# Dense K and Q projections with the padding done by DMA, scores taken from the next pass, and V in three-tile banks

## The chip, the cores and the metric

The kernel runs on one core of a Trainium2 chip. The metric is the device time of one execution in microseconds (us). The kernel before takes 915.73 us, the median of 3 runs (915.34 to 917.61). The engines have short names here: PE is TensorE (matmuls), ACT is ScalarE, DVE is VectorE, POOL is GpSimd, SP is SyncE, which here only issues DMAs.

## The reference

The input x has 2048 tokens of 640 features. The output adds to x the product of an attention branch and a gated branch, both fed by the layer norm of x. The attention has 32 heads of 20 features.

```python
def _A_ref(x, wqkv, wo):
    B, S, D = x.shape
    H = 32; Dh = D // H
    qkv = (x @ wqkv).reshape(B, S, 3, H, Dh).transpose(2, 0, 3, 1, 4)
    q, k, v = qkv[0], qkv[1], qkv[2]
    scores = jnp.einsum("bhqd,bhkd->bhqk", q, k) * Dh ** -0.5
    p = softmax(scores, axis=-1)
    o = jnp.einsum("bhqk,bhkd->bhqd", p, v)
    return o.transpose(0, 2, 1, 3).reshape(B, S, D) @ wo
...
h = sigmoid(xn @ w_gate) * (xn @ w_up)      # 1728 features
g = silu(h @ w_down)
return x + _A_ref(xn, wqkv, wo) * g
```

There are 32 x 2048 x 2048 exponentials to take, some 134 million, against matmuls that are small by comparison, since a head has only 20 features.

## The kernel before, in words

**Layout.** Tokens lie in 16 tiles of 128. xnT holds the normalised x transposed: features on the partitions (5 tiles of 128), tokens along the row. The queries are worked in 4 chunks of 512 and the heads in 8 groups of 4. A *pass* is one chunk of queries with one group of heads, so there are 32 passes. Within a pass the scores of 16 key tiles and 4 heads are computed: 64 *banks*, each a matmul of 128 keys by 512 queries that fills one PSUM bank of 512 f32 columns. The whole kernel has 2048 such banks.

**Padding.** A matmul on 32 of PE's 128 rows works on one head, and four of them run beside each other. So each head gets a strip of 32 partitions: the first row of the strip holds a constant (1 on the side of K, and on the side of Q a bound on the score that keeps the exponentials in range), then 20 rows of features, then 11 rows of zeros. Before the change the padding is in the weights: wkp and wqp hold 32 heads of 32 columns, made on POOL (line 206), and K (line 108) and Q (line 143) are projected group by group, 128 padded columns for 4 heads of 20. The output projection (lines 614, 646) likewise takes the normalised products oT group by group with a padded wo_pad: 8 matmuls for a half of 320 columns. The bound of a group is a matmul with the absolute values of Q (absq, line 127) and the maxima of K (line 121) as weights (line 501).

**The exponentials.** Two engines make them. ACT takes the scores from two PSUM sets, one of 3 banks and one of 2, in turn (line 901); an exponential there is one instruction for the whole set. DVE takes single banks from a *spare* PSUM bank and makes the exponential from integer and cubic steps in four instructions (lines 912, 917, 921, 925: dy, du, du, p), with two buffers for dy and one for du. The probabilities p then go as moving operand into the product with V (line 999), which sums into the PSUM tile oacc, with a column of ones for the softmax's denominator. At a pass's end DVE copies oacc to oev (line 667), POOL's DMAs carry the denominators through DRAM and back, and DVE multiplies (oT, line 696).

**The gated branch.** Gate and up matmuls (lines 541, 554), a tanh on ACT (line 548) for the sigmoid, the down projection (line 576), a tanh (td, line 587) for the silu, and a store to DRAM; out jobs (line 614) read it back (gqr, line 609, four buffers) and add the result onto x in DRAM by an accumulating DMA from POOL. For the last chunk, part jobs (line 646) sum the first six groups before the end, and the last two are added after the last pass.

**What sets the order.** The order of all engines after the setup is planned when the kernel is built, by a loop that keeps its own clock for PE, ACT and DVE. ACT's sets come first: issue() (line 935) lets PE score the next banks as soon as a set is free, or just before ACT would run dry; when DVE has little queued it also gives DVE the next bank, except for the last 6 banks of a pass. Between scores PE does products with V (pv_batch) and *jobs*: K, Q, V, gate and up, down, out and part jobs, each with a due time counted in banks (lines 711 and 725 on), two in flight at most, in two PSUM banks (misc0, misc1) that also serve as spare. A job that is overdue is done before the next scores (must_fill). A zero matmul onto oacc (line 984) fills PE where it would otherwise be idle for long. Changing from one kind of PE work to another is booked with a time of its own (INTO). Every engine executes its instructions strictly in the planned order, and so does SP its DMAs: one that waits holds up those behind it. An SP DMA also waits until the eighth before it has landed.

**The setup** (the first 32 us) loads x, takes the norm, transposes, and projects K of the first group, Q of the first pass and V of four token tiles (16 heads each, line 133, ps_v); a list scheduler orders it.

Of the kernel before, what the change touches and what calls it, by code (L numbers as in the profile page):

```python
# [8 lines left out]
FP32 = mybir.dt.float32  # L9
# [5 lines left out]
P = 128  # L15
HEAD = 32
# [5 lines left out]
V_CHUNKS = ((0, 16), (16, 32))  # L22
# [17 lines left out]
def kernel(  # L40
# [26 lines left out]
    HH = HEAD // 2  # L67
    assert D == 640 and S == 2048 and Dh == 20 and HH * Dh == HALF
# [18 lines left out]
    mk_all = const.tile([P, NG, 4], FP32, name="mk_all")  # L87
    mk = const.tile([P, NG], FP32, name="mk")
    bound = const.tile([P, NG, P], BF16, name="bound")
# [7 lines left out]
    wqp = persist.tile([P, KD, HEAD, 32], BF16, name="wqp")  # L97
    wo_pad = persist.tile([P, NG, D], BF16, name="wo_pad")
# [4 lines left out]
    wkp = ep.tile([P, KD, HEAD, 32], BF16, name="wkp")  # L103
    wv = ep.tile([P, KD, D], BF16, name="wv")

    def k_matmuls(ps, g, cols):
        for kd in range(KD):
            nc.tensor.matmul(ps, lhsT=wkp[:, kd, GH * g:GH * g + GH, :].rearrange("p h e -> p (h e)"),  # L108
                             rhs=xnT[:, kd, cols],
                             start=(kd == 0), stop=(kd == KD - 1))  # L110
            yield

    def k_bound(g):
        k_most(g)
        nc.vector.tensor_scalar(out=bound[:, g, :], in0=esum, scalar1=mk[:, g:g + 1], scalar2=None, op0=ALU.mult)

    def k_most(g):
        nc.vector.tensor_reduce(out=mk[:, g:g + 1], in_=mk_all[:, g, :], axis=AXISX, op=ALU.max)

    def k_max(src, g, c):  # L120
        nc.vector.tensor_reduce(out=mk_all[:, g, c:c + 1], in_=src, axis=AXISX, op=ALU.max,
                                apply_absolute_value=True)

    def q_abs(ps):
        absq = wk.tile([P, QC], BF16, tag="absq", bufs=1, name="absq")
# [5 lines left out]
    def v_matmuls(ps, tt, h0, h1):  # L131
        for kd in range(KD):
            nc.tensor.matmul(ps[:, 0:(h1 - h0) * Dh], lhsT=xnT[:, kd, tt * P:(tt + 1) * P],  # L133
                             rhs=wv[:, kd, h0 * Dh:h1 * Dh], start=(kd == 0), stop=(kd == KD - 1))
            yield

    def v_copy(copy, ps, tt, h0, h1):
        copy(out=v_all[:, tt, h0:h1, 1:1 + Dh],
             in_=ps[:, 0:(h1 - h0) * Dh].rearrange("p (h e) -> p h e", e=Dh))

    def q_matmuls(ps, cols, g):
        for kd in range(KD):
            nc.tensor.matmul(ps, lhsT=wqp[:, kd, GH * g:GH * g + GH, :].rearrange("p h e -> p (h e)"),  # L143
                             rhs=xnT[:, kd, cols],
                             start=(kd == 0), stop=(kd == KD - 1))
            yield

# [3 lines left out]
    with tc.tile_pool(name="setup", bufs=1) as sp, \  # L153
            tc.tile_pool(name="ps0", bufs=1, space=bass.MemoryType.PSUM) as ps0:
        x_sb = sp.tile([P, TT, D], BF16, name="x_sb")
        wk_raw = sp.tile([P, KD, D], BF16, name="wk_raw")
        wq_raw = sp.tile([P, KD, D], BF16, name="wq_raw")
# [20 lines left out]
        load_w(wk_raw, 1)  # L178
        load_x(12, 4)
        load_w(wq_raw, 0)  # L180
# [5 lines left out]
        nc.gpsimd.memset(v_all[:, :, 0:HH, 0:1], 1.0)  # L186
        make_identity(nc, ident)
        nc.vector.memset(wkp[:, :, GH:HEAD, 1 + Dh:32], 0.0)
        for w in (wkp, wqp):
            nc.gpsimd.memset(w[:, :, 0:GH, 0:1], 0.0)  # L190
            nc.gpsimd.memset(w[:, :, 0:GH, 1 + Dh:32], 0.0)
# [13 lines left out]
        def pad_copy(dst, raw, g0, g1):  # L205
            nc.gpsimd.tensor_copy(
                out=dst[:, :, GH * g0:GH * g1, 1:1 + Dh],
                in_=raw[:, :, GH * g0 * Dh:GH * g1 * Dh].rearrange("p k (h e) -> p k h e", e=Dh))
# [38 lines left out]
        def k_mm(c):  # L247
            kps[c] = ps0.tile([P, 512], FP32, tag="k", bufs=KBUFS, name="ps_k")
            for _ in k_matmuls(kps[c], 0, slice(c * 512, (c + 1) * 512)):
                pass  # L250
# [901 lines left out]
```

## Time and profile before

| | |
|---|---|
| median of 3 runs | 915.73 us |
| the profiled execution | 916.7 us, of which the span from its first to its last instruction is 914.8 |
| ACT busy | 880.2 us, 845 instructions |
| DVE busy | 837.8 us, 1424 instructions |
| PE busy | 805.1 us, 6027 matmuls |
| exponentials on ACT | 725, for 1813 banks |
| exponentials on DVE | 235 banks, four instructions each |
| K, Q projections in the passes | 140 and 155 matmuls of 512 columns |
| output projection in the passes | 240 matmuls of 320 columns |
| zero matmuls | 59 |
| PE waits for ACT before scores | 70.4 us in 185 waits |

How to read it: a group's line gives the source line, the engine, what is written and read, the count, the busy time and the mean duration of one, then the idle time of the engine just before and what ended it. A duration runs from an instruction's start to its last write, and the next instruction of the engine may start before that, so durations add up to more than the time they take. The 40 digits of a row in the page are busy shares in tenths, one for each fortieth of the span.

### The profile page before, as it was taken

What the parts mean: (1) busy time and instruction counts of PE and PEld (TensorE: products, weight loads), DVE (VectorE), ACT (ScalarE), POOL (GpSimd) and SP (SyncE); (2) the same over time, 40 slices, a digit from 0 to 9 for tenths busy, and PEclk for the clock granted to TensorE, in tenths of its full rate; (3) what the DMA queues carried; (4) which work ended last, traced back from release to release, by engine and by line L of the source; (5) the groups of instructions that cost most, each with busy time, mean ns of one, the idle gap of its engine ahead of it and who ended that gap; (6) DMA issues with size and microseconds to landing.
All of it is one profiled execution on the core that took longest, in us unless ns stands there. A gap on an engine that the chain in (4) does not pass through costs nothing.

```text
span 914.8 us, 16028 instructions
## 1 busy us (share of the span) xinstructions
PE 805.1 (88%) x6027; PEld 274.3 (30%) x6027; DVE 837.8 (92%) x1424; ACT 880.2 (96%) x845; POOL 167.7 (18%) x307
## 2 busy tenths in 40 slices
PE   5898889988888998898889998998899999989995
PEld 2332223322222233322223333222233322223333
DVE  8799999998999999999999999999889967989995
ACT  6989999999999999999999999999999999999992
POOL 7601111011111111211111112111011221011121
PEclk9999999999999999999999999999999999999997
DMA  6070000002222112322221132322102333220003
GB/s 223 22 227 14 13 14 14 2 14 56 49 64 46 32 59 70 51 56 56 57 49 28 52 100 35 66 62 57 38 20 85 79 49 71 45 56 21 13 17 84
DMA packets 91901, 49.50 MB, mean 54 GB/s; under 512 B 78548, under 2 KB 86132, under 8 KB 91696
## 3 DMA queue, kind: packets, MB, share of 16 engines
q1 hardware_dynamic: 81616, 32.37, 14.0%
q0 software_dynamic: 10208, 16.11, 7.8%
q8 instruction: 47, 0.77, 0.3%
q14 instruction: 30, 0.25, 0.1%
HBM read 40.74 MB, written 9.03 MB: 54 GB/s over the span
## 4 chain that ended last, share of the span: by engine, by line
ACT 64%; issue 16%; DVE 10%; PE 8%; DMA 1%; POOL 0%; SPq 0%; DVEq 0%; ACTq 0%; POOLq 0%
ACT p L901 59%; ACT tnh L548 3%; PE sc L879 3%; DVE dy L912 2%; DVE du L917 1%; DVE du L921 1%; PE work L541 1%; DVE p L925 1%; PE oacc L999 1%; DVE stats L214 1%; PE work L133 1%; PE work L554 1%; ACT td L587 1%; DMA x_sb<-in_A_x_dram 0%; PE work L143 0%
## 5 line engine op out<-in xcount | busy, mean ns | idle before, releaser
L901 ACT ACTIVATE p<-sc 128x1536 bf16<-128x1536 f32 x725 | 840.5, 1399 | 6.6 <-PE oacc L999 5.2
L879 PE MATMUL sc<-qT,kT_all 32*128 32x512 bf16 x1813 | 283.1, 382 | 76.7 <-ACT p L901 70.4
L879 PEld LDWEIGHTS <-kT_all 32*128 32x128 bf16 x2048 | 90.9, 90 | 320.0 <-issue 310.3
L912 DVE TENSOR_SCALAR dy<-spare 128x512 f32<-128x512 f32 x235 | 160.8, 684 | 26.0 <-PE spare L879 23.9
L917 DVE SCALAR_TENSOR_TENSOR du<-dy 128x512 f32<-128x512 uint16 x235 | 161.3, 686 | 4.6
L925 DVE SCALAR_TENSOR_TENSOR p<-du,dy 128x512 uint16<-128x512 f32 x235 | 161.0, 685 | 4.0
L921 DVE SCALAR_TENSOR_TENSOR du<-du,dy 128x512 f32<-128x512 f32 x235 | 161.1, 685 | 3.5
L999 PE MATMUL oacc<-p,v_all 128*21 128x512 bf16 x2048 | 157.4, 383 | 0.0
L668 POOL DMA_DIRECT2D den_dram<-oev x31 | 18.0, 582 | 397.1 <-DVE oev L667 387.8
L879 PE MATMUL spare<-qT,kT_all 32*128 32x512 bf16 x235 | 90.1, 383 | 0.0
L576 PE MATMUL work<-wd,hT 128*128 128x320 bf16 x448 | 85.4, 302 | 0.3 <-DVE dy L912 0.2
L541 PE MATMUL work<-xnT,wg 128*128 128x512 bf16 (+1 forms) x280 | 81.2, 383 | 1.0 <-DVE dy L912 0.3
L554 PE MATMUL work<-xnT,wu 128*128 128x512 bf16 (+1 forms) x280 | 76.7, 381 | 1.8 <-DVE dy L912 0.9
L684 POOL DMA_DIRECT2D rl<-rec_dram x124 | 62.1, 513 | 55.0 <-DMA rec_dram<-den 46.4
L576 PEld LDWEIGHTS <-hT 128*128 128x128 bf16 x448 | 35.7, 97 | 46.9 <-issue 35.3
L999 PEld LDWEIGHTS <-v_all 128*21 128x21 bf16 x2048 | 29.7, 90 | 63.3 <-issue 62.3
L143 PE MATMUL work<-xnT,wqp 128*128 128x512 bf16 x155 | 43.9, 382 | 2.5 <-DVE dy L912 2.0
L548 ACT ACTIVATE tnh<-work 128x512 bf16<-128x512 f32 (+1 forms) x56 | 44.3, 791 | 0.0
L558 DVE SCALAR_TENSOR_TENSOR hT<-tnh,work 128x512 bf16<-128x512 bf16 (+1 forms) x56 | 38.0, 679 | 5.4 <-ACT tnh L548 3.9
L678 POOL DMA_DIRECT2D rec_dram<-den x31 | 17.0, 550 | 132.2 <-DVE den L677 132.2
L108 PE MATMUL work<-xnT,wkp 128*128 128x512 bf16 x140 | 39.8, 383 | 0.9 <-DVE dy L912 0.9
L614 PE MATMUL work<-wo_pad,oT 128*128 128x320 bf16 x192 | 36.1, 302 | 0.7 <-DVE dy L912 0.7
(106 smaller groups left out, 556.1 us busy)
## 6 DMA issues: line engine op xcount, KB each, us to landing
wg<-in_B_w_gate_dram SPq DMA_DIRECT2D x52, 160.0 KB
wu<-in_B_w_up_dram SPq DMA_DIRECT2D x52, 160.0 KB
rl<-rec_dram POOLq DMA_DIRECT2D x124, 64.0 KB, 2.3
gq_dram<-d POOLq DMA_DIRECT2D x12, 320.0 KB, 2.5
gqr<-gq_dram SPq DMA_DIRECT2D x12, 320.0 KB
wd<-in_B_w_down_dram SPq DMA_DIRECT2D x1, 2080.0 KB
out_dram<-in_A_x_dram SPq DMA_DIRECT2D x1, 1920.0 KB
out_dram<-gqr POOLq DMA_DIRECT2D x12, 160.0 KB, 3.7
```

What stands on the lines that cost most here:

```text
L541: nc.tensor.matmul(psg[0:fsz, :], lhsT=wg[:, kd, 0:fsz], rhs=xnT[:, kd, cols], start=(kd == 0), stop=(kd == KD - 1))
L548: nc.scalar.activation(out=made["t"][0:fsz, :], in_=psg[0:fsz, :], func=ACT.Tanh, scale=0.5)
L554: nc.tensor.matmul(psu[0:fsz, :], lhsT=wu[:, kd, 0:fsz], rhs=xnT[:, kd, cols], start=(kd == 0), stop=(kd == KD - 1))
L576: nc.tensor.matmul(psd[:, 0:HALF], lhsT=hT[0:fsz, kf, t4 * P:(t4 + 1) * P], rhs=glu[1][0:fsz, kf, e0_:e1_], start=(kf == 0), stop=(kf == N ...
L684: nc.gpsimd.dma_start(out=t["rl"][32 * j:32 * j + 32, :], in_=rec_dram[n, j:j + 1, :].to_broadcast([32, QC]))
L879: nc.tensor.matmul(ps, lhsT=kT_all[32 * j:32 * j + 32, g, kt * P:(kt + 1) * P], rhs=qTs[qc, g][32 * j:32 * j + 32, :], start=True, stop=Tr ...
L901: nc.scalar.activation(out=buf.tile(), in_=ps, func=ACT.Exp, bias=EXP_BIAS, scale=exp_scale)
L912: nc.vector.tensor_scalar(out=t["y"], in0=ps, scalar1=LEAST, scalar2=None, op0=ALU.max)
L917: nc.vector.scalar_tensor_tensor(out=t["u"], in0=t["f"], scalar=CUBE_2, in1=t["f"], op0=ALU.add, op1=ALU.mult)
L921: nc.vector.scalar_tensor_tensor(out=t["u"], in0=t["u"], scalar=CUBE_1, in1=t["f"], op0=ALU.add, op1=ALU.mult)
L925: nc.vector.scalar_tensor_tensor(out=buf.tile()[:, 0, :].bitcast(U16), in0=t["u"], scalar=CUBE_SCALE, in1=t["y"], op0=ALU.mult, op1=ALU.add)
L999: nc.tensor.matmul(oacc[32 * j:32 * j + 1 + Dh, :], lhsT=v_all[:, b % PER_PASS // GH, GH * g + j, 0:1 + Dh], rhs=buf.ap[:, i, :], start=(n ...
```

## The change

It has seven parts.

1. **K and Q are projected densely.** The 640 features are 5 tiles of 128 columns, without padding, 4 K jobs and 4 Q jobs a tile (wkd, wqd; heads 0 to 3, which the setup still makes in padded form, stand last). DVE copies a K tile to kd, and SP's DMAs move its heads, in pieces of 4 to 20 rows, to their strips in kT_all. The Q tiles go to qd, and pads() moves the pieces of one pass to qT (three buffers) once the scores have come within two passes.
2. **The bounds** of several groups are computed in one bound job: absq now reads qd (bf16 in SBUF) instead of PSUM, the weights have one column a head, and the 32 rows of the result are moved to the strips by a DMA. The row of ones of K's other groups is copied from the first group's by seven DMAs.
3. **The output projection is dense.** After s5 has made oT, SP's DMAs pack its heads into od, and 5 matmuls (4 in part jobs) replace 8 (6). wo is loaded as it is; only the last two groups keep a padded copy, wo_end. gqr has two buffers instead of four, and the last chunk's gated values lie in kT_all.
4. **Banks of the next pass.** Each of the four heads has its own count of banks scored. ACT takes the lowest ones that are open, and in the last 6 banks of a pass DVE gets a bank of the next pass.
5. **V** is projected for heads 0 to 7 with three token tiles in a bank, then 8 to 15 in the same way, then 16 to 31 as before; the setup makes heads 0 to 7 of four tiles.
6. **DVE's exponential** has two buffers for du, and the plan books its steps with 606 ns and 114 more for a step that depends on the one before.
7. **The plan's constants**: a change to scores is booked with 100 instead of 160 ns, and the due times of K and Q are earlier. A score reads 21 rows of a strip instead of 32.

The core of the diff:

```diff
-V_CHUNKS = ((0, 16), (16, 32))
+VF = 8
+V_PARTS = ((0, VF, 3), (VF, 16, 3), (16, 32, 1))
+DENSE = 5
...
-            nc.tensor.matmul(ps, lhsT=wkp[:, kd, GH * g:GH * g + GH, :].rearrange("p h e -> p (h e)"),
-                             rhs=xnT[:, kd, cols],
+    def dense_matmuls(ps, w, t, cols):
+        for kd in range(KD):
+            nc.tensor.matmul(ps, lhsT=w[:, kd, ROWS + P * t:ROWS + P * (t + 1)], rhs=xnT[:, kd, cols],
                              start=(kd == 0), stop=(kd == KD - 1))
...
-        absq = wk.tile([P, QC], BF16, tag="absq", bufs=1, name="absq")
+        absq = wk.tile([P, QC], BF16, tag="absq", bufs=2, name="absq")
...
-            op(("v", t), "PE", 0.8, [("xnT", t), "wv"], lambda t=t: v_mm(t), 1.0)
+            op(("v", t), "PE", 0.4, [("xnT", t), "wv"], lambda t=t: v_mm(t, 1), 1.0)
...
-    INTO = {"score": 160.0, "pv": 100.0, "fill": 100.0}
+    INTO = {"score": 100.0, "pv": 100.0, "fill": 100.0}
...
+        def evict():
+            made["k"] = ep.tile([P, 512], BF16, tag="kd", bufs=2, name="kd")
+            nc.vector.tensor_copy(out=made["k"], in_=ps)
+            for h, r, d, n in pieces(t):
+                g, j = divmod(h, GH)
+                if g:
+                    nc.sync.dma_start(out=kT_all[32 * j + 1 + d:32 * j + 1 + d + n, g, cols], in_=made["k"][r:r + n, :])
+            landed[t, c] = dve.t + DMA_WAIT
...
+        qd_cells[qc, t] = dve.add(606.0, [Cell(pe[0] + PE_OUT)], lambda: nc.vector.tensor_scalar(
+            out=qd[:, t, :], in0=ps, scalar1=q_scale, scalar2=None, op0=ALU.mult), 1)
...
+    def pads():
+        n = next_pad[0]
+        if n == NQC * NG or front() < PER_PASS * (n - 2):
+            return False
...
+        qT = wk.tile([P, QC], BF16, tag="qT", bufs=3, name="qT")
+        for t in TILES[g]:
+            for h, r, d, k in pieces(t):
+                if h // GH == g:
+                    at_row = 32 * (h % GH) + 1 + d
+                    nc.sync.dma_start(out=qT[at_row:at_row + k, :], in_=qd[r:r + k, t, :])
+        row = (g - 1) % NG * GH
+        nc.sync.dma_start(out=qT[0:P:32, :], in_=b_tiles[qc, g][row:row + GH, :])
...
-        gqr = glu[0].tile([P, D], FP32, tag="gqr", bufs=4, name="gqr")
+        gqr = glu[0].tile([P, D], FP32, tag="gqr", bufs=2, name="gqr")
...
-            for g in range(NG):
-                nc.tensor.matmul(pss[:, 0:HALF], lhsT=oTs[qc, g][:, t4 * P:(t4 + 1) * P],
-                                 rhs=wo_pad[:, g, h * HALF:(h + 1) * HALF], start=(g == 0), stop=(g == NG - 1))
+            for k in range(KD):
+                nc.tensor.matmul(pss[:, 0:HALF], lhsT=ods[qc][:, k, t4 * P:(t4 + 1) * P],
+                                 rhs=wo_all[:, k, h * HALF:(h + 1) * HALF], start=(k == 0), stop=(k == KD - 1))
...
+                    nc.sync.dma_start(out=ods[qc][a % P:a % P + b - a, a // P, :], in_=oT[at_row:at_row + b - a, :])
...
-    K_DUE, Q_DUE, V_DUE, OUT_DUE = -40, -24, 6, 4 * PER_PASS
+    K_DUE, Q_DUE, B_DUE, V_DUE, OUT_DUE = -60, -50, -36, 6, 4 * PER_PASS
...
+    def coming(n):
+        return sorted(b for b in map(bank_of, range(GH)) if b < NB)[:n]
...
+    def dve_bank(banks):
+        b = min((x for x in coming(GH) if x not in banks), default=None)
...
+        left = PER_PASS - b % PER_PASS
+        if left > (NEEDED if b < NB - PER_PASS else NEEDED_LAST):
+            return b
...
+        b = PER_PASS * (b // PER_PASS + 1) + b % GH
...
-            t["u"] = pp.tile([P, 512], FP32, tag="du", bufs=1, name="du")
+            t["u"] = pp.tile([P, 512], FP32, tag="du", bufs=2, name="du")
...
-        first = dve.add(600.0, [Cell(begun + MM5 + PE_OUT - 100.0), *d_made[-2:-1]], bits, 0)
-        c = dve.add(610.0, [first, *d_made[-1:]], square, 3)
+        first = dve.add(606.0, [Cell(begun + MM5 + PE_OUT - 100.0), *d_made[-2:-1]], bits, 0, 114.0)
+        c = dve.add(606.0, [first, *d_made[-2:-1]], square, 3, 114.0)
...
+    for g in range(1, NG):
+        nc.sync.dma_start(out=kT_all[0:P:32, g, :], in_=kT_all[0:P:32, 0, :])
```

## The prediction

> **What bounds the kernel now.** I read the page's busy shares and slices first, then the chain that ended last, then the groups of ScalarE (ACT) by form, then its timeline.
>
> ```profile
> span 914.8 us, 16028 instructions
> ...
> PE 805.1 (88%) x6027; PEld 274.3 (30%) x6027; DVE 837.8 (92%) x1424; ACT 880.2 (96%) x845; POOL 167.7 (18%) x307
> ...
> ACT  6989999999999999999999999999999999999992
> ...
> PEclk9999999999999999999999999999999999999997
> ...
> ACT 64%; issue 16%; DVE 10%; PE 8%; DMA 1%; POOL 0%; SPq 0%; DVEq 0%; ACTq 0%; POOLq 0%
> ```
>
> ACT is busy in every slice after the first two and leads the chain; TensorE (PE) has its full clock throughout. So the end is set by how much ACT has to do, how often it waits, and what stands before its first and after its last exponential. The groups by form give the work, the timeline its true rate:
>
> ```profile
> L901 ACT ACTIVATE p<-sc 128x1536 bf16<-128x1536 f32 x363 | 585.1, 1612 | 3.7 <-PE oacc L999 2.5 <-POOL wqp L206 1.2
> L901 ACT ACTIVATE p<-sc 128x1024 bf16<-128x1024 f32 x362 | 428.9, 1185 | 3.0 <-PE oacc L999 2.6 <-PE sc L879 0.2
> ```
> ```profile
> 300.97 0.84 ACT L548 ACTIVATE tnh<-work 128x512 bf16<-128x512 f32 x1
> 301.45 5.80 ACT L901 ACTIVATE p<-sc 128x1024 bf16<-128x1024 f32 x5
> ...
> 307.35 18.08 ACT L901 ACTIVATE p<-sc 128x1536 bf16<-128x1536 f32 x16
> 325.68 0.74 ACT L587 ACTIVATE td<-d 128x640 bf16<-128x640 f32 x1 [0.25 <-DVE d L580]
> ```
>
> The means overlap: the next one starts some 0.28 us before the last has ended. Sixteen exponentials (eight pairs of 3 and 2 banks) take 18.08 - 0.28 = 17.8 us, 2.23 us a pair. The forms differ by 1612 - 1185 = 427 ns, so one of 3 banks holds ACT for 1.33 us and one of 2 for 0.90. A tanh holds it 301.45 - 300.97 = 0.48, a td about 0.63. From the first exponential (32.36) to the end of the last (896.6) are 864.3 us; the work is 363 x 1.33 + 362 x 0.904 + 56 x 0.48 + 16 x 0.63, about 847. ACT therefore waits about 17 us in all, 4.3 of them early:
>
> ```profile
> 32.36 18.37 ACT L901 ACTIVATE p<-sc 128x1536 bf16<-128x1536 f32 x16 [1.15 <-POOL wqp L206]
> 52.67 3.71 ACT L901 ACTIVATE p<-sc 128x1536 bf16<-128x1536 f32 x3 [1.94 <-PE oacc L999]
> ```
> ```profile
> 50.00:100.00 50.00, 43.68 (x331) 14.24 (x328) 49.28 (x88) 45.68 (x41) 5.51 (x10) 1.00 0.32 104
> ```
>
> (The last four busy times are PEld, VectorE (DVE), ACT, POOL behind PE: ACT 45.68 of 50.)
>
> **The change, part by part.** The counts are those of the two programs' instruction orders; they are fixed when the kernel is built.
>
> *ACT's work.* DVE makes 256 banks of probabilities instead of 235, ACT 1792 instead of 1813: 358 of 3 banks and 359 of 2. That is 5 x 1.33 + 3 x 0.90 = **9.4 us less**, straight on the path.
>
> *The first exponential.* It starts at 32.36, 0.49 after its scores at 31.87. Those stood behind fifteen V matmuls:
>
> ```profile
> 29.74 2.20 PE L133 MATMUL ps_v<-wv,xnT 128*128 128x320 bf16 x15
> ```
>
> Now ten of half that width stand there, some 0.7 us, done before qT (30.6). With scores at about 30.7 and ACT free at about 31.1, the first exponential starts near 31.2: **1.1 us less** (the page's POOL wqp was over at 32.25 too; no copy of that kind is left).
>
> *The end.* The part jobs stood on it:
>
> ```profile
> 896.48 0.61 PE L999 MATMUL oacc<-p,v_all 128*21 128x512 bf16 x8
> 897.03 1.80 PE L646 MATMUL work<-wo_pad,oT 128*128 128x320 bf16 x12
> ...
> 899.27 0.68 DVE L1080 COPY oev<-oacc 128x512 f32<-128x512 f32 x1
> ```
>
> The last product into oacc is done near 897.1, but oev is copied only at 899.27, behind the last part products. With 4 matmuls in place of 6 per half, all 32 part matmuls now stand well ahead of the last scores: **2.0 us less** (2.2 at most). What follows oev keeps its instructions.
>
> *DVE, which pays for ACT's relief.* A step of an exponential on DVE is 685 ns in the groups, but what counts is from start to start:
>
> ```profile
> 300.00 0.69 DVE L921 SCALAR_TENSOR_TENSOR du<-du,dy 128x512 f32<-128x512 f32 x1
> 300.72 0.69 DVE L925 SCALAR_TENSOR_TENSOR p<-du,dy 128x512 uint16<-128x512 f32 x1
> ...
> 303.25 0.69 DVE L912 TENSOR_SCALAR dy<-spare 128x512 f32<-128x512 f32 x1
> 303.85 0.68 DVE L667 COPY oev<-oacc 128x512 f32<-128x512 f32 x1
> ```
>
> 0.72 when a step follows the one it reads, 0.60 when an unrelated one follows. In the order before, 248 steps stand directly behind their own predecessor, in the order after 139 (du has two buffers). Before: 940 x 0.60 + 248 x 0.12 = 594, and some 198 of other work (means less 0.08 overlap), 792 of ACT's 864 us. After: 1024 x 0.60 + 139 x 0.12 = 631. Of the other work, 31 qT evictions at 744 ns, 31 absq at 677, 28 K evictions at 742 and their 28 maxima at 676 become 20 qd, 20 kd and 20 maxima of 0.60, 8 rows of 0.60, and 24 absq that read bf16 from SBUF. No row has such an absq: 0.17 by the 254 ns of the 128-column bound, 0.60 if it runs like its PSUM form; I take 0.3, since four times the columns must cost more than the bound and its two-byte operands are that row's. V is 16 copies of 0.40 and 9 of about 0.58 in place of 28. Together about 172, the sum 803 of some 853: 94% where it was 92%. I count it at nothing; the cover is 50 us.
>
> The Trainium skill speaks against that sum (VectorE: DVE Perf Modes, The DRAIN you can't avoid): the next operation waits until the pipe is empty, and operations without semaphores between them were no faster. By it a second du would gain nothing; 0.72 and 0.60 in this trace say otherwise.
>
> *PE.* K has 40 matmuls less, Q 55, the bound 7, each 0.216 (three of 512 columns take 0.82, the last 0.38); the output products 88 less of 0.136 (the twelve above take 1.80, the last 0.30); V costs 1.6 us more; 103 more zero products give 22 back: 10 us less in all, beside 70.4 us in which PE waited for ACT. A switch to scores is now booked at 100 instead of 160 ns, so scores may come 60 ns later. The trace has about 0.1 for it (three gate-and-up matmuls from 300.84, the next scores at 301.59 = 300.84 + 3 x 0.216 + 0.10). Cost: nothing if slack remains; 32 us if all 540 rounds in which PE did not wait for ACT pay 60 ns. ACT is busy 50.00 of 50 us in eleven of the windows, so I take **+1.5**.
>
> *DMAs.* SP gets some 420 more issues: K, Q and O move between the dense and the padded layout in pieces of 4 to 20 rows. 32 comparable ones took 11.90 us:
>
> ```profile
> 37.71 11.90 SPq L754 DMA_DIRECT2D wo_pad<-in_A_wo_dram  x32
> ```
>
> 0.37 each, 155 us of an SP that mostly waited. In the view of DMA issues small ones land in 1.7 us (den_dram) to 2.3 (rl), so a qT of six takes about 4.5. In the order it is asked for 22 banks before pass 1, 16 before pass 2, 50 and more from pass 4 on (864 us / 2048 = 0.42 a bank: 9, 7, over 20 us); before it was 4 to 50 banks, with 4 at passes 2 and 6. K's first 28 pieces (10.4 us of issuing, behind 16 other DMAs) are the tightest: 0 to 3 us at pass 1. So are gqr's loads, which now have two buffers and wait for the accumulating DMA two tiles back, 0 to 1 us at three places. The first wg, wu and wd, issued from 49.66 on before, now stand in SP's order behind K's pieces, after an O move that DVE makes 34 banks (14 us) ahead of the first gate matmul: nothing, or a landing of 2 to 4 us once if SP is late. I take **+1.0** for all three. The Trainium skill warns of such transfers (DMA: Bandwidth & Descriptors, Rules for kernel authors: below 64 KB one pays mostly overhead); by it the overhead would matter only where nothing runs ahead, which is pass 1.
>
> *Waits that go.* Early on K, Q and V had to be done in a hurry; PE has less of it now, and Q is asked for sooner. Of the 17 us I take **3.5 back** (0 to 7).
>
> Sum: -9.4 - 1.1 - 2.0 + 1.5 + 1.0 - 3.5 = -13.5 us. The profiled execution took 916.7 (span 914.8 and 1.9 around it), 1.0 above the median 915.7: 903.2 by the one, **902** by the other.
>
> **The rivals.**
> - *Scores come late* (the 60 ns): a third of the 540 rounds pay in full, 11 us in place of 1.5: 911. For it: 540 of 725 rounds; against: the measured switch is 0.1.
> - *Pieces land late*: pass 1 and the three chunk ends wait 2 us more each: 910. For it: 28 pieces in a row; against: the leads above.
> - *DVE becomes the bound, slower than before.* Place: the four steps of each bank. If two interleaved chains still start 0.72 apart, DVE needs 1024 x 0.72 + 172 = 909 us for a stream of 853, and the time is 902 + 56 = 958. It decides from 50 us over the sum; from 64 over, the kernel is slower. For it: 94% leaves little room; against: 0.60 in the trace. The Trainium skill's rule, weighed above, would give this result.
> - *The waits merely move* and eat the gain: within 0.3%, 915.
>
> **How the numbers follow.** Forecast 0.68 (894 to 908), late scores 0.12, late pieces 0.07, waits move 0.03, DVE bound 0.10. The measurement tells 0.3% (2.7 us) from no change. Faster 0.87, same 0.03, slower 0.10. The range 894 to 912 takes in the two milder rivals and leaves out the dearer one; below 894 ACT would have to lose more than half its waits.
>
> **What would show it.** ACT: 717 exponentials, about 802 us by starts, and waits of 13 to 17 us; the first one near 31.2; oev within 1 us of the last product into oacc. DVE steps of two chains 0.60 apart and DVE 93 to 96% busy. SP's pieces landed before the first score of their pass, pass 1 above all. Wrong if PE waits for dy, du or a qT in many passes, or if ACT's waits exceed 25 us.

## The result, and the profile after

The changed kernel takes **965.89 us** (median of 4 runs, 959.80 to 968.62), the kernel before beside it 915.54: a ratio of 1.054 with an interval of 1.048 to 1.059. The forecast was 902 in a range of 894 to 912, so both the time and the sign were wrong. The profiled execution took 963.62. Medians and ratios in this document leave out the slow runs, over 1.5% above the same kernel's fastest: one of e2's four (957.09) and two of e10's ten (931.63, 934.43).

The page of the profile after, in the lines that answer to those of before:

```profile
span 961.7 us, 16771 instructions
...
PE 828.2 (86%) x6020; PEld 275.9 (29%) x6020; DVE 841.9 (88%) x1475; ACT 875.3 (91%) x837; POOL 159.0 (17%) x306
...
PEclk9888987999899997999999979999999999979997
...
ACT 47%; issue 16%; PE 15%; DVE 12%; SPq 5%; DMA 4%; DVEq 0%; POOL 0%; ACTq 0%; POOLq 0%
...
L492 DVE CAST kd<-work 128x512 bf16<-128x512 f32 x20 | 13.7, 684 | 29.3 <-DMA kT_all<-kd 25.4
```

ACT's busy time is 5 us less, as the plan wanted, but it is busy for 91% of the span and not 96. In the chain that ended last its share falls from 64% to 47%, and DMA and SP's queue, 1% and nothing before, now hold 9%. The clock row, which is the clock that the chip granted to PE, has dips. And the eviction of a K tile to kd, a step of 13.7 us in all, was preceded by 25.4 us in which DVE waited for the transfers out of kd.

To measure ACT's waits I take the time from each of its instructions' start to the next one's, less the median of its form (1.331 us for 3 banks, 0.904 for 2, 0.478 for a tanh, 0.627 for a td), and sum it. Before: **16.9 us**. After: **77.2 us**, of which 45 stand before 250 us, 8 near 370, 10 near 560, and the rest in a few places behind. Elsewhere it is 0.1 to 0.8 us in 25, as before. The sum of the differences closes: first exponential at 30.55 where it was 32.36 (-1.8), ACT's work -9.4, waits +60.3, and 16.0 us from the end of the last exponential to the end of the span where it was 18.2 (-2.2): 46.9, and the spans differ by 46.9.

**The largest hole** is 12 us long, in pass 0. These are ACT's, PE's and DVE's timelines there, each line with the idle time before it:

```profile
53.64 1.45 ACT L1055 ACTIVATE p<-sc 128x1536 bf16<-128x1536 f32 x1 [11.69 <-PE sc L1032]
```
```profile
47.08 0.58 PE L1032 MATMUL spare<-qT,kT_all 21*128 21x512 bf16 x1 [6.95 <-DVE kd L492]
...
52.41 0.59 PE L120 MATMUL work<-xnT,wqd 128*128 128x512 bf16 x1 [4.21 <-DMA kT_all<-kd]
```
```profile
46.34 0.69 DVE L492 CAST kd<-work 128x512 bf16<-128x512 f32 x1 [8.04 <-DMA kT_all<-kd]
51.66 0.69 DVE L492 CAST kd<-work 128x512 bf16<-128x512 f32 x1 [3.44 <-DMA kT_all<-kd]
```

Read from below: DVE stands 8.04 us before the third K eviction, since kd has two buffers and the pieces that read the first have not landed. PE waits 6.95 us for the bank that this eviction empties; the Q matmul at 52.41 is put down to the transfers, but it is the next eviction, which they held until 51.66, that empties its bank. Both engines work in order, so scores that need nothing of K's stand behind them too, and ACT is dry for 11.69 us. Why the pieces come so late is in SP's timeline:

```profile
39.75 21.16 SPq L496 DMA_DIRECT2D kT_all<-kd  x28
61.01 2.98 SPq L597 DMA_DIRECT2D qT<-qd  x4
64.09 0.56 SPq L599 DMA_DIRECT2D qT<-row  x1
```

28 pieces took 21.16 us to issue, **0.756 each**, where the forecast had 0.37. And qT of pass 1 is behind them. The price is not all of it: the first K tile was evicted at 32.10, but SP has 16 other DMAs to issue until 39.66. An estimate from these rows: at 0.37 the first tile's seven pieces would have been out at 42.3 instead of 45.1, and DVE, done with other work at 38.3, would still have stood some 5 of the 8.04 us.

**The later holes** are at the chunk ends. DVE, then SP:

```profile
566.34 0.49 DVE L714 SCALAR_TENSOR_TENSOR gqr<-work,gqr 128x320 f32<-128x320 f32 x1 [6.00 <-DMA gqr<-gq_dram]
```
```profile
555.65 3.04 SPq L803 DMA_DIRECT2D od<-oT  x4
558.80 3.58 SPq L597 DMA_DIRECT2D qT<-qd  x5
562.42 0.56 SPq L599 DMA_DIRECT2D qT<-row  x1
563.09 0.37 SPq L703 DMA_DIRECT2D gqr<-gq_dram  x1
```

gqr's load is issued at 563.09, behind ten pieces that began 7.4 us earlier; DVE gets it at 566.34 and has stood 6.00 us.

### The profile page after: what moved, and what is told of

Same layout as the page of the kernel before. It is cut to its first block, busy times and chain, and to the rows that moved or that the text cites. A ratio compares the mean times of both kernels' runs of the same rounds, so it can differ in the third digit from the quotient of the medians.

```text
span 961.7 us, 16771 instructions
## 1 busy us (share of the span) xinstructions
PE 828.2 (86%) x6020; PEld 275.9 (29%) x6020; DVE 841.9 (88%) x1475; ACT 875.3 (91%) x837; POOL 159.0 (17%) x306
## 4 chain that ended last, share of the span: by engine, by line
ACT 47%; issue 16%; PE 15%; DVE 12%; SPq 5%; DMA 4%; DVEq 0%; POOL 0%; ACTq 0%; POOLq 0%
ACT p L1055 42%; PE sc L1032 5%; SPq L496 3%; ACT tnh L641 3%; DVE dy L1066 3%; PE oacc L1158 2%; DVE du L1075 2%; DVE du L1071 2%; DVE p L1079 2%; PE work L120 1%; PE work L634 1%; DMA gqr<-gq_dram 1%; PE work L150 1%; DMA kT_all<-kd 1%; DMA den<-den_dram 1%
## 5 line engine op out<-in xcount | busy, mean ns | idle before, releaser
L1032 PE MATMUL sc<-qT,kT_all 21*128 21x512 bf16 x1792 | 288.5, 394 | 70.5 <-ACT p L1055 64.6
L1066 DVE TENSOR_SCALAR dy<-spare 128x512 f32<-128x512 f32 x256 | 175.3, 685 | 40.1 <-PE spare L1032 37.8
L1032 PEld LDWEIGHTS <-kT_all 21*128 21x128 bf16 x2048 | 91.4, 91 | 324.5 <-issue 312.8
L1075 DVE SCALAR_TENSOR_TENSOR du<-du,dy 128x512 f32<-128x512 f32 x256 | 174.5, 683 | 2.1
L1079 DVE SCALAR_TENSOR_TENSOR p<-du,dy 128x512 uint16<-128x512 f32 x256 | 174.2, 681 | 1.9
L1071 DVE SCALAR_TENSOR_TENSOR du<-dy 128x512 f32<-128x512 uint16 x256 | 174.2, 683 | 1.1
L1032 PE MATMUL spare<-qT,kT_all 21*128 21x512 bf16 x256 | 101.3, 396 | 10.8 <-DVE kd L492 10.7
L764 POOL DMA_DIRECT2D den_dram<-oev x31 | 17.9, 579 | 426.6 <-DVE oev L763 426.6
L1143 PE MATMUL oacc<-xnT,zero 128*128 128x512 bf16 x162 | 57.2, 399 | 0.0
L120 PE MATMUL work<-xnT,wqd 128*128 128x512 bf16 x100 | 34.0, 447 | 14.5 <-DVE gqr L714 9.7
L492 DVE CAST kd<-work 128x512 bf16<-128x512 f32 x20 | 13.7, 684 | 29.3 <-DMA kT_all<-kd 25.4
```

What stands on the lines that cost most here:

```text
L1032: nc.tensor.matmul(ps, lhsT=kT_all[32 * j:32 * j + 1 + Dh, g, kt * P:(kt + 1) * P], rhs=qTs[qc, g][32 * j:32 * j + 1 + Dh, :], start=True, ...
L1066: nc.vector.tensor_scalar(out=t["y"], in0=ps, scalar1=LEAST, scalar2=None, op0=ALU.max)
L1071: nc.vector.scalar_tensor_tensor(out=t["u"], in0=t["f"], scalar=CUBE_2, in1=t["f"], op0=ALU.add, op1=ALU.mult)
L1075: nc.vector.scalar_tensor_tensor(out=t["u"], in0=t["u"], scalar=CUBE_1, in1=t["f"], op0=ALU.add, op1=ALU.mult)
L1079: nc.vector.scalar_tensor_tensor(out=buf.tile()[:, 0, :].bitcast(U16), in0=t["u"], scalar=CUBE_SCALE, in1=t["y"], op0=ALU.mult, op1=ALU.add)
```

## The experiments

Theory A: SP issues a piece from SBUF to SBUF in 0.75 us, twice what the forecast assumed, and the plan takes a transfer to land 3.4 us after DVE's step, however long SP's queue is; DVE, PE and ACT then wait in order behind late pieces (kd's buffers, qT, gqr), and each hole is followed by a lower clock. Rivals: B, DVE has too much to do with two banks in turn; C, scores come 60 ns late; D, the landings as such are late; G, the clock falls by itself. In the table "waits" are ACT's, as above, in the profiled run, which need not be the median one (e6's is its slowest, 918.01, and e7's, 906.81, is among its three fastest); the ratio is to the kernel before in the same session.

| | median us | ratio, interval | waits us |
|---|---|---|---|
| before | 915.54 to 916.69 | 1 | 16.9 |
| after | 965.89 | 1.054, 1.048 to 1.059 | 77.2 |
| e1 eight kd buffers | 946.14 | 1.034, 1.030 to 1.038 | 59.1 |
| e2 K's pieces on POOL | 945.71 | 1.032, 1.028 to 1.036 | 59.3 |
| e3 wide K pieces | 923.63 | 1.009, 1.006 to 1.012 | 35.5 |
| e4 four gqr buffers | 962.75 | 1.047, 1.041 to 1.053 | 79.8 |
| e6 = e3 + early gqr | 911.00 | 0.994, 0.992 to 0.996 | 26.1 |
| e7 = e6 + large loads cut | 912.55 | 0.993, 0.990 to 0.996 | 18.9 |
| e8 = e7, scores booked 160 | 911.62 | 0.995, 0.993 to 0.996 | 25.8 |
| e9 = e7 + more zeros | 904.75 | 0.987, 0.985 to 0.988 | 17.9 |
| e10 = e7, one du | 914.52 | 0.997, 0.995 to 1.000 | 27.4 |
| e11 = e1 + e2 | 940.68 | 1.025, 1.023 to 1.028 | 52.2 |
| e12 before + more zeros | 917.44 | 1.002, 1.001 to 1.003 | 17.1 |
| e13 after + more zeros | 952.77 | 1.039, 1.035 to 1.044 | 62.5 |

### e1: eight buffers for kd

```diff
-            made["k"] = ep.tile([P, 512], BF16, tag="kd", bufs=2, name="kd")
+            made["k"] = ep.tile([P, 512], BF16, tag="kd", bufs=8, name="kd")
...
-        done = dve.add(606.0, [Cell(pe[0] + PE_OUT), *kd_free[-2:-1]], evict, 1)
+        done = dve.add(606.0, [Cell(pe[0] + PE_OUT), *kd_free[-8:-7]], evict, 1)
```

> One part: the K tiles that VectorE evicts and SP's pieces read get eight buffers where the changed kernel has two; every instruction keeps its place in its engine's order, so only waits can differ. Theory A (SP spends 0.75 us on a piece from SBUF to SBUF, VectorE's next eviction waits in order for those pieces, PE and ScalarE wait behind it, and the clock drops after each hole): the 25.4 us that VectorE waits before the eviction to kd go almost wholly; K's pieces themselves and the qT behind them still come late, so of the 50 us that ScalarE waits above its row's pace before 250 us some 15 to 30 go: 935 to 950 us. Rival B (two approximated banks in turn load VectorE too much): the waits stay where they are, 960 to 968. Rival C (scores put 60 ns late each round): as B, 960 to 968. Rival D (the pieces' landing, not the wait of VectorE, is what ScalarE waits for): VectorE's wait goes but turns into PE's wait on kT_all and qT, 958 to 966.

946.14. As A said, DVE's 25.4 us are gone; what is idle before the eviction now is 2.1 us, and it ends by PE. Some 20 us of the time went with it, so B and C fall as the main cause: ACT, DVE, SP and, by its weight loads, PE execute the same instructions in the same order as in the changed kernel. The rest of the delay turned into PE's wait for qT:

```profile
65.83 0.58 PE L1032 MATMUL sc<-qT,kT_all 21*128 21x512 bf16 x1 [9.58 <-DMA qT<-row]
```

SP still needs 21.1 us for the first 28 pieces, and qT's stand behind them.

### e2: K's pieces on POOL

```diff
-                    nc.sync.dma_start(out=kT_all[32 * j + 1 + d:32 * j + 1 + d + n, g, cols], in_=made["k"][r:r + n, :])
+                    nc.gpsimd.dma_start(out=kT_all[32 * j + 1 + d:32 * j + 1 + d + n, g, cols], in_=made["k"][r:r + n, :])
```

> One part: the 140 pieces of K are issued by POOL where the changed kernel issues them by SP; two buffers of kd stay. Theory A: what matters is one queue's issuing rate, so taking 105 us of issuing from SP leaves qT, od and gqr on time (their share of the waits goes, some 10 us), and K's pieces go out at POOL's rate, which the profile shows as 0.50 us for each of the four copies of rl: 7 pieces in 3.5 us rather than 5.3; VectorE's wait before kd falls from 25.4 us to some 8: 925 to 945 us. If POOL takes 0.75 us or more for such a piece: 945 to 960. Rivals B and C: 960 to 968.

945.71, a little over A's 945. POOL issues the same pieces 0.50 us apart (14 in 7.00 us), and DVE's wait before kd falls to 6.1 us. A piece lands 1.7 us after its issue in the median (1.6 to 5.1), so the landings as such are mostly as short as was forecast. (The trace has 128 such pieces, and 32 wide ones in e3, where the expectations say 140 and 35.) Why the time fell no further is told by e11.

### e3: wide pieces

```diff
+            if c == 0:
+                kd_tiles[t] = ep.tile([P, S], BF16, tag="kd", bufs=2, name="kd")
+            made["k"] = kd_tiles[t][:, cols]
...
+            if c < 3:
+                return
...
-                    nc.sync.dma_start(out=kT_all[32 * j + 1 + d:32 * j + 1 + d + n, g, cols], in_=made["k"][r:r + n, :])
+                    nc.sync.dma_start(out=kT_all[32 * j + 1 + d:32 * j + 1 + d + n, g, :], in_=kd_tiles[t][r:r + n, :])
+            for x in range(4):
+                landed[t, x] = dve.t + 8000.0
...
-            jobs.append(Job(k_job(t, c), K_COST, 0, PER_PASS * (1, 2, 4, 5, 7)[t] + K_DUE + 2 * c, True, True))
+            jobs.append(Job(k_job(t, c), K_COST, 0, PER_PASS * (1, 2, 4, 5, 7)[t] + K_DUE - 8 + 2 * c, True, True))
```

> K's pieces made wide: a K tile of 128 rows is evicted into one buffer of 2048 columns, and one piece per head and tile, 20 rows of 4 KB, takes the place of four of 1 KB: 35 issues rather than 140. The planner's order shifts with it. Theory A: SP's time for K falls from 105 us to 35 x 0.75 = 26 us if the price goes by the rows (to some 35 x 1.5 = 52 if half of it goes by the bytes), VectorE's wait before kd goes, and of the 50 us of ScalarE's waits before 250 us some 35 to 45 go: 915 to 930 us. Rivals B and C: 960 to 968. Rival D: if it is the landing, the wide pieces land later than narrow ones and passes 1, 2 and 4 wait more: over 950.

923.63, as A said; D falls as the main cause. SP's timeline, with the second line a tile that it did not wait for:

```profile
40.91 6.25 SPq L500 DMA_DIRECT2D kT_all<-kd  x7
...
69.83 5.15 SPq L500 DMA_DIRECT2D kT_all<-kd  x7
```

0.74 us for a piece of 80 KB where one of 20 KB took 0.756: the price is for the transfer, not for its bytes. ACT's waits before 250 us fall from 45 to 8 us. This one edit takes back 42 of the 50 us. It does three things at once: fewer pieces, a landing booked at 8 us instead of 3.4, and K's jobs due 8 banks earlier. What each brought was not tried apart.

### e4: four buffers for gqr

```diff
-        gqr = glu[0].tile([P, D], FP32, tag="gqr", bufs=2, name="gqr")
+        gqr = glu[0].tile([P, D], FP32, tag="gqr", bufs=4, name="gqr")
...
```

> One part: gqr gets four buffers, as in the kernel before, where the changed kernel has two (room is made by putting the setup's bound matrix among the setup's tiles). Theory A: the waits of VectorE on gqr (11.7 us) and of PE behind it (9.7 us) go, and with them ScalarE's holes near 370 and 560 us, 8 and 10 us long with their trails; what stands before 250 us stays: 945 to 953 us. Rivals B and C: 960 to 968. If gqr is late because its load stands behind other pieces of SP rather than for want of a buffer: the second tile's wait stays, 955 to 963.

962.75, within the spread of the changed kernel. My reading of the buffers was wrong: DVE still stands 6.03 us before gqr at 577.12, and SP issues that load at 573.84, behind the pieces of od and qT. The place in the queue is what makes it late.

### e5: the price of an issue

> Leaves the whole computation out: it fills the output with a copy of x and issues transfers alone, eight of a kind one behind the other and none that waits for another's landing: on SP 20 rows of 1 KB from SBUF to SBUF and from DRAM to SBUF, then 8, 16, 64, 128 and 32 rows from SBUF, 128 from DRAM, 20 rows of 4 KB from SBUF, 20 rows to DRAM; on POOL 20 rows from SBUF, 20 from DRAM, 128 from SBUF; on ScalarE 20 rows from SBUF. The times of the issuing instructions are what is asked for. Theory A (the kind of transfer sets SP's price): 0.75 us for 20 rows from SBUF to SBUF, 0.37 for 20 rows from DRAM, 0.75 for 4 KB rows too, and 0.50 on POOL. Rival E (the rows or the 16 transfer engines set it): 0.65 for 8 rows, 0.75 for 20, over 1 us for 64 and 128, whichever memory the rows come from. Rival F (SP's price rises because the queue is full or the kernel's other transfers press on it): here, with nothing else running, 20 rows from SBUF go out at 0.37 us as the rows of DRAM do.

SP's timeline (eight of a kind a line; a, c, f and w go from SBUF to SBUF with 20, 8, 128 rows of 1 KB and 20 of 4 KB, b and g from DRAM to SBUF with 20 and 128, scratch from SBUF to DRAM with 20):

```profile
11.60 6.15 SPq L68 DMA_DIRECT2D a<-src  x8
17.79 3.15 SPq L70 DMA_DIRECT2D b<-in_A_wqkv_dram  x8
20.98 5.40 SPq L72 DMA_DIRECT2D c<-src  x8
...
36.53 5.10 SPq L78 DMA_DIRECT2D f<-src  x8
41.67 3.93 SPq L80 DMA_DIRECT2D g<-in_A_wqkv_dram  x8
...
50.70 6.08 SPq L84 DMA_DIRECT2D w<-src  x8
56.82 3.75 SPq L86 DMA_DIRECT2D scratch<-src  x8
```

From one start to the next, in the median, it is 0.75 us for 20 rows from SBUF to SBUF and 0.38 for the same rows from DRAM, on an SP with nothing else to do. POOL was issuing beside a and b, but w, with no other engine issuing, costs 0.75 too: F falls. The row count alone does not set the price either, as E has it: 128 rows cost less (0.64) than 20, though 8 cost 0.67. The source alone does not: 20 rows from SBUF to DRAM start 0.34 to 0.37 us apart in four of seven steps (the others take 0.56 to 0.79). It is SBUF at both ends that is dear: 0.63 to 0.75 us in all seven kinds tried, against 0.34 to 0.47 with DRAM at one end. POOL takes 0.50 to 0.55 for each of the three kinds tried. ScalarE's eight take 10.11 us, but four of the seven steps between them are 0.75 to 0.76, as on SP; what holds the others for 1.3 to 2.6 was not looked into.

### e6, e7: gqr early, and the large loads cut

```diff
-        gqr = glu[0].tile([P, D], FP32, tag="gqr", bufs=2, name="gqr")
-        nc.sync.dma_start(out=gqr, in_=gq_dram[tt, :, :])
-        landed = Cell(pe[0] + 3000.0)
+        gqr, landed = gqrs[tt]
+        yield "wait", [landed]
...
+    def gqr_ahead():
+        tt = next_gqr[0]
...
+        if all(c is not None and c.t is not None and c.t + 6000.0 <= pe[0] for c in (made, left)):
+            load_gqr()
```
```diff
-        nc.sync.dma_start(out=wd[:, 0:nf, :], in_=B_w_down[0:nf * P, :].rearrange("(f p) d -> p f d", p=P))
...
+        for k, (dst, part) in enumerate(parts):
+            at(pe[0] + 8000.0 * (k + 1), lambda dst=dst, part=part: nc.sync.dma_start(out=dst, in_=part))
```

> The wide pieces of K, and gqr loaded as soon as its rows are written and a buffer is free (four buffers, the planner takes 8 us for the landing and takes no bank before it), where the load stood behind od's and qT's pieces on SP. Theory A: the waits of VectorE on gqr (10.7 us with wide pieces alone) and PE's and ScalarE's behind it go, at all three chunk ends: of the wide pieces' 35.5 us of ScalarE's waits some 15 to 19 go, 923.6 to 904 to 910 us. Rivals B and C: no change from 923.6. If the holes come from the late jobs themselves and not from gqr's load: 918 to 924.

> As e6, and the transfers of w_down (2.1 MB) and of x to the output (1.9 MB), issued in one go at the start of the gate and up products, are cut into seven pieces 8 us apart, so that the four qT pieces behind them, 7.5 us of SP's time with wide pieces, go out at 0.75 us each. Theory A: the hole near 205 us (3.9 us) goes: 901 to 907 us, under the kernel before. Rival B or C: as e6 or slower. If the large transfers only press somewhere else: as e6.

e6: 911.00, 13 us below e3; the holes at the three chunk ends are gone. It missed its range by 1 us; in its profiled run, the slowest of the five, new waits stand near 500, 605 and 880 us, each behind a fall of the granted clock. e7: 912.55, over its range of 901 to 907 and not to be told from e6 (its runs lie from 900.74 to 913.99), though the hole near 205 us went (3.9 us of waits to 0.3). It was not a wait for qT, as A had it. At this place of the changed kernel DVE stands 4.31 us, until 237.78, for the denominators: their transfer, issued at 232.0 just after the large loads, lands after 5.75 us where the median is 1.97. In e6 it takes 5.28, and DVE's stand of 1.32 us is followed by a fall of the clock; in e7 it takes 3.63 and DVE does not stand. In the profiled run the longest waits now follow a fall of the clock; the windows read us, then busy time of PE, PEld, DVE, ACT, POOL, the clock, and DMA (share, GB/s):

```profile
485.00:490.00 5.00, 3.22 (x30) 1.23 (x30) 4.97 (x9) 4.73 (x6) 1.27 (x3) 1.00 0.31 84
490.00:495.00 5.00, 5.00 (x31) 1.40 (x27) 4.45 (x9) 4.68 (x4) 0.95 (x2) 0.60 0.45 134
495.00:500.00 5.00, 5.00 (x27) 1.14 (x26) 2.19 (x4) 2.75 (x3) 1.40 (x3) 0.50 0.12 26
```

The trace shows PE busy for 3.22 of 5 us; then its clock is halved until about 508 us, and in that time PE is busy almost without a break and ACT starves (2.75 of 5).

### e8: scores booked at 160 ns again

```diff
-    INTO = {"score": 100.0, "pv": 100.0, "fill": 100.0}
+    INTO = {"score": 160.0, "pv": 100.0, "fill": 100.0}
```

> As e7, with the planner's INTO of scores at 160 again, as in the kernel before, so scores are put 60 ns earlier against the end of ScalarE's work. Rival C (late scores are what the change lost): 3 us or more under e7. Theory A: within 3 us of e7 either way, as ScalarE's steady stretches wait 0.1 to 0.5 us in 25 in both kernels.

911.62 beside 912.55: no difference that e7's spread of 13 us would let one see. C falls as a cause of tens of us; a cost of 1 or 2 us is not excluded.

### e9, e12, e13: more products of zeros

```diff
-    WINDOW, ENOUGH = 3400.0, 2300.0
+    WINDOW, ENOUGH = 3400.0, 2800.0
```

> As e7, with the planner's ENOUGH at 2800 where it was 2300: PE is kept at work for 2.8 us of each 3.4 with products of zeros into oacc (356 of them where e7 has 154). Of e7's 18.9 us of ScalarE's waits some 9 stand between 475 and 570 us, where the granted clock is 0.50 to 0.69 for 20 us after PE sat for 1.8 us. Theory A's clause on the clock (a hole is followed by half the clock, and the late work by a trail of small waits): with 0.25 us less of idle time in each us and no fall of the clock, 8 to 10 us of the waits go in every run, and the runs, 900.7 to 914.0 in e7, draw together: median 897 to 904. Rival G (the clock falls on its own, whatever PE does): the spread stays, median 905 to 914. If the zeros stand in the way of scores: 0.1 us later in some rounds, 910 to 920.

> The kernel before with ENOUGH at 2800 where it was 2300: 210 products of zeros where it had 59. It is the control of e9. Its granted clock is 0.994 as it is and ScalarE's waits are 16.9 us, so by theory A the zeros bring it nothing, 913 to 919 us, and what e9 gains on it, 11 us, comes from the dense projections with their transfers mended and not from the zeros. Rival H (e9's gain is the zeros'): 903 to 909.

> The changed kernel with ENOUGH at 2800 alone (350 products of zeros where it had 162). Its holes are PE's in-order waits for VectorE and for transfers, in which no product of zeros can run either, so theory A keeps the holes (about 45 us of the 77 us of ScalarE's waits) and the half clock that follows each; only falls of the clock without a hole go: 955 to 966 us. Rival G2 (the fall of the clock is the main loss, and the holes are its effect): 915 to 935.

e9: **904.75**, four runs within 3.3 us, 1.3% below the kernel before, whose runs beside it begin at 915.24; DVE is busy 93% of its span and ACT 97%. The clock row of its page:

```profile
PEclk9999999999999999999999999999999999899998
```

The median lies 0.75 us over A's range, and one fall of the clock is left near 785 us (4.4 us of waits). e12 is the control: the same setting makes the kernel before no faster (1.002), so e9's gain on it is the change's own, with its transfers mended and its clock kept up. e13: 952.77, 13 us under the changed kernel and 2 under A's range. The plan's order shifts with the setting, so the 13 us are not the clock's alone. But the changed kernel's fall at 841.91 has no wait of PE over 0.95 us in the 8 us before it: my clause says that a hole is followed by half the clock, and half the clock comes without one too; but the holes stand (21.6 us before kd, 62.5 us of waits), and G2 is far off.

### e10: one buffer for du

```diff
-            t["u"] = pp.tile([P, 512], FP32, tag="du", bufs=2, name="du")
+            t["u"] = pp.tile([P, 512], FP32, tag="du", bufs=1, name="du")
...
```

The costs of the four steps in the plan are those of the kernel before.

> As e7, with the tile du of the approximated bank in one buffer and the planner's costs of its steps as in the kernel before, so that the steps of one bank follow each other directly; VectorE takes 251 banks where e7 gives it 254. Rival B says that two banks in turn bring VectorE nothing or load it too much: then e10 is as e7 or faster, 900 to 912. Theory A: two in turn are 0.60 us apart and one alone 0.72, so VectorE has up to 251 x 3 x 0.12 = 90 us more to do, beyond the 8% that it is idle, and where other work doesn't lie between the steps ScalarE waits for banks: 915 to 940 us.

914.52, just under A's range and over B's, and e7's runs overlap it: no verdict between A and B on the time. Between 250 and 460 us the last step is followed after 0.72 us in the median, with two buffers after 0.60. DVE is busy 849 us where e7 has 836, so the second du saves 13 us of DVE's time; that ACT hardly feels it, since other work lies between the steps, is likely but not shown.

### e11: e1 and e2 together

> The changed kernel with both parts of e1 and e2: eight buffers for K's tiles, and K's pieces issued by POOL. PE, VectorE and ScalarE have the order of the changed kernel. Theory A: VectorE's wait before the eviction to kd goes (25.4 us in the changed kernel, none in e1) and so does the lateness of qT behind K's pieces on SP; what stays are the holes at the start of the gate and up products and at the three chunk ends, as with the wide pieces (35 us of waits in all), and some at pass 1, where POOL takes 14 us for the 28 pieces: 922 to 935 us. Rival D (the landings as such are late, whoever issues): 940 to 948, as e1 and e2 alone.

940.68, above A's range and in D's; e3 had refuted D as the main cause. DVE's and POOL's timelines show what I had left out:

```profile
72.22 0.25 DVE L773 RECIPROCAL den<-den 128x16 f32<-128x16 f32 x1 [3.34 <-DMA den<-den_dram]
```
```profile
63.20 7.08 POOL L496 DMA_DIRECT2D kT_all<-kd  x14 [0.59 <-DVE kd L492]
70.28 0.57 POOL L769 DMA_DIRECT2D den<-den_dram  x1
```

On POOL K's pieces stand ahead of the denominators' transfers, and DVE, in order again, waits at the reciprocal (3.34 us here, 3.50 at 135.61; in e2 2.18, 3.08 and 5.32). This is theory A in another queue: the planner counts neither. The other waits, at the first gate job and the chunk ends, are like those of e3.

## Why the prediction was wrong

**What failed** is the term "DMAs", put at +1.0 us "for all three". ACT's waits rose by 60 us where the forecast had them fall by 3.5, and nearly all of that hangs on this term: the edits that mend K's and gqr's transfers (e3, e6) take back 55 us, with what the clock gains by them.
- *The price.* "0.37 each" came from 32 rows-to-strips transfers out of DRAM; the new ones start in SBUF and take 0.756. K's first 28 cost 21.2 us, not 10.4. e5 shows that the ends make the difference: it is dear from SBUF to SBUF, and not from SBUF to DRAM.
- *The missed wait.* kd's two buffers make DVE's in-order eviction wait for SP. The prediction named the wait for gqr, and a late qT, and none for kd. It priced what SP would issue and not who stands behind it. e1: 20 us for this alone. Of the two errors this is the deeper one: at the forecast's price the first wait would still have been some 5 us, by the estimate above.
- *The leads.* "22 banks before pass 1" counts from the place where the program issues qT; SP reached it 28 pieces later. A lead in the program is worth what the queue ahead of it leaves.
- *gqr* was named with the right places, but for the wrong reason (buffers; e4), and at 0 to 1 us each: e6 gave 13 us for the three.
- The first gate loads were named, "a landing of 2 to 4 us once". The place was right, but what landed late there, and held DVE for 4.31 us, was the denominators' transfer behind the large loads (see e7).
- *The clock* was in no step. It was 0.994 before and 0.947 after; asking for more products of zeros, which raises it, brought 8 us on e7 (e9) and 13 on the changed kernel (e13).

The rival "pieces land late" (7%, 910 us) had the right places, pass 1 and the three chunk ends, but at 2 us each: it has the same price, and DVE's wait at kd is not in it either.

The Trainium skill's rule that the prediction weighed (DMA: Bandwidth & Descriptors, Rules for kernel authors) is that transfers under 64 KB are mostly overhead. The traces agree as far as issuing goes: pieces of 20 and of 80 KB cost SP the same 0.75 us. My gloss, that it would matter in pass 1 alone, was wrong: the holes at the chunk ends are of the same kind. The Trainium skill says on the same page (Issuing engines are not separate DMA queues) that a second issuing engine saves only the issuing time, usually small beside the transfer. Here it was not small: 28 pieces took 21.16 us to issue, and one lands 1.7 us after its issue (e2).

**What held.** ACT's work: 717 exponentials, 801 us by starts. The first exponential at 30.55 (forecast near 31.2), and the end: oev 0.48 us after the last exponential and a tail 2.2 us shorter (forecast 2.0):

```profile
946.23 0.69 DVE L1242 COPY oev<-oacc 128x512 f32<-128x512 f32 x1 [2.99 <-PE oacc L1158]
```

DVE is no bound: steps of two banks start 0.60 us apart, absq takes 284 ns (forecast 0.3), and between 400 and 550 us ACT is busy 149.85 of 150. e8 shows no cost of the scores' 60 ns, though the 1.5 us of the forecast would be lost in its spread. The 3.5 us of early waits that were to go are seen in e9: before 200 us ACT waits 3.9 us there and 7.8 in the kernel before. With the transfers and the clock mended, e9 runs in 904.75, and 902 had been forecast: the other steps of the sum, taken together, were about right, and what SP and the clock took was worth 61 us.

**Why the clock falls where PE has no long hole** can be read from the granted clock of the 14 profiles. Within a run every stretch at half clock starts a whole number of slots of 3.41 us after the first one, and lasts 1 to 10 such slots if the end does not cut it off. So I put each run on its grid of 3.41 us, from 35 us after its start to 25 us before its end, and summed PE's busy time in each slot at full clock:

| PE busy in the slot | slots | followed by half clock |
|---|---|---|
| under 2.11 us | 56 | 56 |
| 2.11 to 2.47 us | 79 | 13 |
| over 2.47 us | some 3,200 | 0 |

It is PE's idle time in a slot, summed, that counts, and not the longest wait: before the fall at 876 us in e6 no wait of PE is longer than 0.57 us. That slot and the next (columns as in e7's windows):

```profile
872.92:876.33 3.41, 2.40 (x19) 0.96 (x18) 3.41 (x7) 3.41 (x4) 1.49 (x2) 1.00 0.06 9
876.33:879.74 3.41, 3.41 (x18) 0.71 (x17) 2.31 (x5) 2.49 (x3) 2.01 (x4) 0.50 0.71 160
```

This speaks against G. The plan's ENOUGH of 2.3 us lies within the doubtful middle row, e9's 2.8 above it. (Some matmul records are missing from the traces, so the bounds are rough.) The Trainium skill (TensorE: Matmul & The Clock Gate, HAM oscillation) warns of idle gaps above some 3.4 us. In e7 a half clock followed where the longest wait was 1.78 us, so here less is enough.

**Open:** what ends a stretch at half clock, since slots with PE busy throughout are followed by more of it as often as not; how the 50 us divide between late transfers and the clock that falls after them; and what e7's cut of the large loads is worth.

## What to carry to other kernels

Price a DMA's issue from a row of the same kind, source and destination alike, multiply it by the number in a row, and treat the issuing queue as an engine with its own clock; then list every in-order engine that waits for a buffer those transfers free, and ask when the queue gets to their first one. Fewer and longer transfers are the first remedy: four times the bytes cost the same issue. When work is taken from PE, look whether its clock holds: sum its idle time over short windows, and do not look for long holes alone.

## What the runs showed of the hardware

- Issue prices, from one start to the next (e5). SP: 20 rows from SBUF to SBUF 0.75 us, 8 rows 0.67, 16 to 128 rows 0.63 to 0.64; from DRAM to SBUF 0.38 for 20 rows and 0.47 for 128; from SBUF to DRAM 0.34 to 0.37 for 20 rows in four of seven steps. POOL: 0.50 to 0.55 for the three kinds tried. ScalarE: 0.75 to 0.76 for 20 rows from SBUF to SBUF where nothing held it.
- PE's clock is halved after a slot of 3.41 us in which PE was busy for less than 2.11 us (56 of 56), never after one with more than 2.47 us, and for a multiple of 3.41 us: 17 us in e7, 34 in e10. More products of zeros keep it up: 0.977 in the median of e7's runs, 0.992 in e9's.
- A transfer of the denominators landed after 5.75 us with loads of 2.1 and 1.9 MB issued just ahead, where 1.97 is the median.
